# Denominators of block 2 on GpSimd and a re-timed side program in an attention + two-MoE kernel

## The chip, the cores and the metric

The kernel runs on one core of one Trainium2 chip. The metric is the device time of one execution in microseconds (us). Three runs of the kernel before gave 718.23, 719.92 and 720.44 us; the median is 719.92 us.

## What is computed

Three layers follow each other, all in float32; the reference, cut to what matters:

```python
# 1: linear attention, 4 batches x 8 heads x 576 tokens, head size 64, 128 features
proj = x @ w_phi                                   # for q and for k
proj = proj - max(abs(proj), axis=-1)
phi  = concat([exp(proj), exp(-proj)])             # s = 0 and s = 1 below
kv, z = k_phi.T @ v, sum(k_phi)
y = (q_phi @ kv) / (q_phi @ z + 1e-6)              # num / den
# 2: gated MLP over 2304 tokens, d_model 512, d_ff 1536
xn = y / sqrt(mean(y * y, -1) + 1e-6) * rms_g
o  = (silu(xn @ w_gate) * (xn @ w_val)) @ w_out
# 3: soft MoE, 8 experts x 4 slots, over the 2304 rows of o
logits = o @ phi
slots  = experts(softmax(logits, axis=0).T @ o)
out    = softmax(logits, axis=1) @ slots
```

## The kernel before

**Stages of the program.** First all of k and v are reduced to kv and z per batch and head, with the q side of block 0 in between (class Rows). Then comes the main loop: six blocks of 384 tokens. For each block b, twelve steps m compute a gate tile (pg), a value tile (pv) and add three output tiles (acc); every gate and value tile is 12 matmuls, because each operand is split into a high and a low part. Last come the experts (y) and the combination (op).

**The side program.** Beside the MoE of block b run the q side of block b+1 and the slot steps of block b-1, cut into small functions. Each m has three fill points, so a block has fills 0 to 35. Tables of fill numbers say where each function is issued: TURNED1 for the q side of block 1, REDUCED for block 2, ADDED for blocks 3 to 5, PSLOTS for the slot steps. A scheduler then orders the instructions of each engine; from block 2 on `placed` pins VectorE's order to the order of issue.

**Three ways to do the q side.** Turned (block 1): tokens in the rows; the projection (P) is turned by TensorE (T) and exponentiated; pairs of heads give the sums num and the denominators den on TensorE. Reduced (block 2): the projection is qP (two matmuls), GpSimd takes the largest magnitude across partitions (L308), VectorE subtracts it (L312), ScalarE takes both exponentials (L313, L314), and num and den are matmuls again (L223, L251). Added (blocks 3 to 5): num as before, but the denominator is weighted on ScalarE and VectorE (L351, L352) and summed across partitions by GpSimd (L353), one call per head; norm (L371 to L375) divides. num takes, for a pair of heads, first both heads' s = 0, then both heads' s = 1: the two heads write different halves of the rows.

**The mean square.** For blocks 1 and 2 scale makes three one-column matmuls (ssq, L269) from s, the sum of squares, then a reciprocal root, a diagonal dg (L274), and spreads it: for block 1 by a matmul (r, L439), for block 2 by GpSimd (L321). For blocks 3 to 5 GpSimd sums the squares across partitions (total, L381) and transposes on VectorE (L385, L364) make and spread the root. out (L282) multiplies into xraw, and split_block casts it to xnh and xnl (L121, L124) for the next block's MoE.

**Slot steps** (post): three turns (x2tp), logits (LT), rows (L), dturn (dtp), dispatch (sps), combine (VectorE) and cturn (ctp).

**Memory.** Block 0's loop still converts the last nine weight pieces in a pool of its own (conv); block 2's q pool is opened when block 1's loop begins.

Of the kernel before, what the change touches and what calls it, by code (L numbers as in the profile page):

```python
# [7 lines left out]
F32 = mybir.dt.float32  # L8
# [3 lines left out]
ALU = mybir.AluOpType  # L12
# [4 lines left out]
NB, NH, SEQ, HD, DF = 4, 8, 576, 64, 128  # L17
NT, DM, DFF = 2304, 512, 1536
# [17 lines left out]
CEVERY = 3  # L36
PSLOTS = [1, 4, 7, 12, 14, 16, 18, 20, 24]
REDUCED = [0, 0, 2, 3, 5, 6, 4, 8, 7, 11, 12, 9, 14, 12, 17, 18, 15, 20, 18, 23, 24, 27, 30]
ADDED = [-3, -3, -1, 0, 2, 3, 6, 1, 5, 4, 8, 9, 12, 6, 11, 9, 14, 15, 18, 12, 17, 15, 20, 21, 25, 26, 28, 31]
TURNED0 = [2, 8, 14, 20, 12, 15, 20, 26, 28, 33]  # L40
TURNED1 = [0, 7, 14, 21, 6, 13, 20, 26, 29, 31]

# [25 lines left out]
def tile_kernel(ctx: ExitStack, tc: tile.TileContext, q2T, qT, kT, v, wbd, wg, wv, wo, rmsg, phi, w1, w2, consts, out):  # L68
# [30 lines left out]
    qctx = ctx.enter_context(ExitStack())  # L99
# [6 lines left out]
    ident = cst[:, 0:128]  # L106
# [98 lines left out]
    class Q:  # L205
# [35 lines left out]
        def attend(self, c):  # L241
# [22 lines left out]
            self.next_kv(c)  # L264

        def scale(self):
            ssq = self.psum("ssq", [128, TPB])
            for i in range(TPB):
                PE.matmul(out=ssq[:, i:i + 1], lhsT=self.s[:, 128 * i:128 * i + 128], rhs=ones_sb[:, 0:1], start=True, stop=True)  # L269
            ms = self.sp.tile([128, TPB], F32, tag="ms", name="ms", bufs=1)  # L270
            DVE.tensor_scalar(out=ms, in0=ssq, scalar1=1.0 / DM, scalar2=1e-6, op0=ALU.mult, op1=ALU.add)
            rsqrt(self.sp, ms)
            dg, r = self.spare()
            DVE.tensor_tensor(out=dg.rearrange("p (i t) -> p i t", i=TPB),  # L274
                              in0=ident.rearrange("p (o t) -> p o t", o=1).to_broadcast([128, TPB, 128]),
                              in1=ms.rearrange("p (i o) -> p i o", o=1).to_broadcast([128, TPB, 128]), op=ALU.mult)
            self.r = self.spread(r, dg)

# [5 lines left out]
    class Reduced(Q):  # L284
# [31 lines left out]
        def spare(self):  # L316
            e = self.sp.tile([128, 2, BLK], F32, tag="e", name="dg", bufs=4)
            return e[:, 0], e[:, 1]

        def spread(self, r, dg):  # L320
            POOL.partition_all_reduce(r, dg, channels=128, reduce_op=bass_isa.ReduceOp.add)  # L321
            return r

        def begin(self):
            self.pair = {}
            for h in range(3):
                self.load(h)

        def steps(self):
            def first():  # L330
                self.split(0)
                self.load(3)

            f = [lambda h=h: self.feature(h) for h in range(NH)]
            a = [lambda c=c: self.attend(c) for c in range(4)]
            g = [lambda h=h: self.exps(h) for h in range(NH)]
            s = [first, *(x for c in range(4) for x in (f[2 * c], f[2 * c + 1], g[2 * c], g[2 * c + 1], a[c])), self.scale, self.out]
            return sorted(zip(REDUCED, s), key=lambda x: x[0])

    class Added(Reduced):  # L340
# [14 lines left out]

        def few(self, name, x, scale, add):

            f = self.sp.tile([128, BLK // 32, 1], F32, tag=name, name=name, bufs=1)
            DVE.tensor_scalar(out=f, in0=x.rearrange("p (b j) -> p b j", j=32)[:, :, 0:1], scalar1=scale, scalar2=add, op0=ALU.mult, op1=ALU.add)
            return f  # L360

        def many(self, out, f):

            DVE.transpose(out=out.rearrange("p (b j) -> p b j", j=32), in_=f.to_broadcast([128, BLK // 32, 32]))  # L364

        def norm(self, c):
# [9 lines left out]
            self.square(c, y, e[0][:, 1])  # L376

        def total(self):
            e = self.sp.tile([128, 2, BLK], F32, tag="e", name="ss", bufs=4)
            self.ss = e[:, 0], e[:, 1]  # L380
            POOL.partition_all_reduce(self.ss[0], self.s, channels=128, reduce_op=bass_isa.ReduceOp.add)  # L381

        def scale(self):
            ss, self.r = self.ss
            DVE.transpose(out=self.r, in_=ss)  # L385
            ms = self.few("ms", self.r, 1.0 / DM, 1e-6)
            f = ms.rearrange("p b o -> p (b o)")
            rsqrt(self.sp, f, BLK // 32)
            self.many(self.r, ms)

# [12 lines left out]
    class Turned(Q):  # L403
# [29 lines left out]
        def spare(self):  # L433
            e = self.sp.tile([128, 2, 2, BLK], F32, tag="e", name="dg", bufs=self.bufs["e"])
            return e[:, 0, 0], None

        def spread(self, r, dg):
            r = self.psum("r", [128, BLK])
            PE.matmul(out=r, lhsT=ones_sb[:, 0:1].to_broadcast([128, 128]), rhs=dg, start=True, stop=True)  # L439
            return r  # L440

# [3 lines left out]

        def steps(self, at, attend, end, lag=2):


            r, pr = [], {}

            def p(c, i):
                pr[c, i] = self.project(c, i)

            for c in range(4):
                for i in range(TPB):
                    r.append((at[c] + i, lambda c=c, i=i: p(c, i)))
                    r.append((at[c] + i + lag, lambda c=c, i=i: self.turn(c, i, pr[c, i])))
                r.append((attend[c], lambda c=c: self.attend(c)))
            r += [(end[0], self.scale), (end[1], self.out)]
            return sorted(r, key=lambda x: x[0])  # L460
# [283 lines left out]
    with ExitStack() as p2:  # L744
# [483 lines left out]
```

## Time and profile before

| | |
|---|---|
| runs (us) | 718.23, 719.92, 720.44 |
| profiled execution | 719.95 us, of which the span of the program on the core is 718.0 us |
| TensorE busy | 702.5 us, 98% of the span |
| VectorE, ScalarE, GpSimd busy | 453.2, 340.8, 125.3 us |
| granted TensorE clock, mean of the span | 0.994 |

PE is TensorE, PEld its weight loads, DVE VectorE, ACT ScalarE, POOL GpSimd, SP the queue that issues DMAs; L223 is line 223 of the kernel before. In a timeline a row stands for a run of like instructions: start, duration from the first one's start to the last one's end, engine, line, operation, out<-in, shapes, count, and in brackets the idle time before it and who ended it. A float32 matmul is recorded as two instructions, so four num matmuls of 384 columns read as x8. Matmuls overlap: the start of the next row tells more than the end of this one.

### The profile page before, as it was taken

How to read it: one execution, taken by the hardware profiler on the slowest of the kernel's cores; microseconds unless marked ns; L12 is line 12 of the kernel's file. 1: busy time of each engine (PE TensorE's matmuls, PEld its weight loads, DVE VectorE, ACT ScalarE, POOL GpSimd, SP SyncE). 2: the span in 40 equal slices, each digit the busy share in tenths (PEclk: the TensorE clock that was granted, in tenths of full speed). 3: DMA queues.
4: the chain of work that ended last, by engine and by line, in shares of the span. 5: the costliest groups of instructions: out<-in, count | busy, mean ns of one | idle time of the engine just before them, and what ended most of it. 6: DMA issues, size and time to landing. Idle time of an engine off the chain costs nothing.

```text
span 718.0 us, 11949 instructions
## 1 busy us (share of the span) xinstructions
PE 702.5 (98%) x4729; PEld 574.2 (80%) x4729; DVE 453.2 (63%) x889; ACT 340.8 (47%) x715; POOL 125.3 (17%) x66
## 2 busy tenths in 40 slices
PE   7999999999999999999999999999999999999995
PEld 4666667888889888888879888899887999988443
DVE  4889995999575564656766667766666663243313
ACT  4878886788444554454441555414444231112103
POOL 0000000000002110125542244432443400000100
PEclk9999999999999999999999999999999999999998
DMA  6755534551011100100000100001000057467898
GB/s 227 269 183 180 186 128 147 188 187 60 1 64 44 34 23 12 39 23 22 23 1 9 44 23 24 1 9 35 21 1 1 9 234 294 176 252 283 316 365 287
DMA packets 25143, 79.43 MB, mean 111 GB/s; under 512 B 2688, under 2 KB 13376, under 8 KB 18688
## 3 DMA queue, kind: packets, MB, share of 16 engines
q1 hardware_dynamic: 24720, 77.52, 30.6%
q10 hardware_dynamic: 368, 1.15, 0.5%
q8 instruction: 37, 0.61, 0.3%
q14 instruction: 18, 0.15, 0.1%
HBM read 71.99 MB, written 6.67 MB: 110 GB/s over the span
## 4 chain that ended last, share of the span: by engine, by line
PE 95%; ACT 2%; DMA 1%; DVE 1%; issue 0%; SPq 0%; ACTq 0%
PE pv L954 22%; PE pg L954 21%; PE acc L979 7%; PE acc L980 7%; PE acc L981 7%; PE kacc L573 5%; PE num L223 5%; PE P L528 3%; PE kacc L582 3%; PE y L1116 2%; PE y L1100 2%; PE o L474 1%; PE P L414 1%; DMA wraw<-in_wo_dram 1%; PE x2tp L763 1%; PE den L251 1%
## 5 line engine op out<-in xcount | busy, mean ns | idle before, releaser
L954 PE MATMUL pv<-xnh,wv 128*128 128x384 f32 x576 | 152.8, 346 | 0.0
L954 PE MATMUL pg<-xnh,wg 128*128 128x384 f32 x576 | 150.2, 342 | 0.3 <-ACT xnh L121 0.3
L954 PEld LDWEIGHTS pv<-xnh,wv 128*128 128x128 f32 x576 | 102.6, 188 | 12.3 <-issue 7.5
L308 POOL PARTITION_ALL_REDUCE qe<-qe x32 | 51.3, 1602 | 334.5 <-ACT qe L307 334.5
L954 PEld LDWEIGHTS pg<-xnh,wg 128*128 128x128 f32 x576 | 104.6, 188 | 5.7 <-ACT xnh L121 0.7
L954 PE MATMUL pg<-xnl,wg 128*128 128x384 f32 x288 | 97.5, 339 | 0.0
L954 PE MATMUL pv<-xnl,wv 128*128 128x384 f32 x288 | 97.5, 339 | 0.0
L979 PE MATMUL acc<-wo,hh 128*128 128x512 f32 x216 | 88.9, 412 | 0.0
L980 PE MATMUL acc<-wo,hh 128*128 128x512 f32 x216 | 85.7, 397 | 0.0
L981 PE MATMUL acc<-wo,hl 128*128 128x512 f32 x216 | 85.5, 396 | 0.0
L962 DVE SCALAR_TENSOR_TENSOR t<-t,pg 128x384 f32<-128x384 f32 x72 | 39.7, 551 | 71.1 <-ACT t L961 70.9
L121 ACT CAST hh<-t 128x384 fp32r<-128x384 f32 x72 | 36.9, 513 | 96.2 <-PE acc L980 74.9
L124 DVE TENSOR_TENSOR hl<-t,hh 128x384 fp32r<-128x384 f32 x72 | 40.6, 564 | 53.5 <-ACT hh L121 44.4
L353 POOL PARTITION_ALL_REDUCE qe<-qe x24 | 61.9, 2626 | 71.3 <-DVE qe L352 41.8
L961 ACT ACTIVATE t<-pg 128x384 f32<-128x384 f32 x72 | 35.3, 490 | 66.0 <-PE pg L954 65.9
L966 DVE TENSOR_TENSOR t<-t,pv 128x384 f32<-128x384 f32 x72 | 39.5, 548 | 30.1 <-PE pv L954 29.5
L954 PEld LDWEIGHTS pg<-xnl,wg 128*128 128x128 f32 x288 | 54.0, 188 | 0.5 <-DVE xnl L124 0.3
L954 PEld LDWEIGHTS pv<-xnl,wv 128*128 128x128 f32 x288 | 54.1, 188 | 0.4 <-issue 0.3
L981 PEld LDWEIGHTS acc<-wo,hl 128*128 128x128 f32 x216 | 40.6, 188 | 10.0 <-DVE hl L124 0.3
L979 PEld LDWEIGHTS acc<-wo,hh 128*128 128x128 f32 x216 | 40.7, 189 | 7.9 <-ACT hh L121 0.9
L980 PEld LDWEIGHTS acc<-wo,hh 128*128 128x128 f32 x216 | 40.7, 189 | 6.4
L573 PE MATMUL kacc<-kp,vt 128*64 128x256 f32 (+1 forms) x320 | 41.2, 393 | 2.3 <-ACT kp L550 2.3
(218 smaller groups left out, 1060.9 us busy)
## 6 DMA issues: line engine op xcount, KB each, us to landing
eu<-in_w_dram SPq DMA_DIRECT2D x32, 1024.0 KB, 6.3
wraw<-in_wg_dram SPq DMA_DIRECT2D x6, 1024.0 KB, 4.8
wraw<-in_wv_dram SPq DMA_DIRECT2D x6, 1024.0 KB, 5.5
wraw<-in_wo_dram SPq DMA_DIRECT2D x6, 1024.0 KB, 5.1
qraw<-in_qT_dram SPq DMA_DIRECT2D x32, 192.0 KB, 2.3
vt<-in_v_dram SPq DMA_DIRECT2D x18, 256.0 KB, 3.3
out_dram<-ob SPq DMA_DIRECT2D x18, 256.0 KB, 2.9
raw<-in_kT_dram SPq DMA_DIRECT2D x17, 256.0 KB, 3.1
```

The source lines that it names most:

```text
L121: ACT.copy(out=hi, in_=src)
L124: (lo_eng or POOL).tensor_tensor(out=lo, in0=src, in1=hi.bitcast(F32), op=ALU.subtract)
L223: PE.matmul(out=num[64 * hh:64 * hh + 64, t0:t1], lhsT=kvt[b][:, 2 * c + hh, s, 0:HD], rhs=e[hh][:, s, t0:t1], start=s == 0, stop=s == 1, ...
L308: POOL.partition_all_reduce(e[:, 0], e[:, 1], channels=128, reduce_op=bass_isa.ReduceOp.absmax)
L353: POOL.partition_all_reduce(e[hh][:, 1], u, channels=128, reduce_op=bass_isa.ReduceOp.add)
L573: PE.matmul(out=kva[o0:o0 + 64, hh // 2], lhsT=self.vt[r0:r1, h], rhs=kp[r0:r1, hh].rearrange("p s f -> p (s f)"), start=first and hh < 2, ...
L954: PE.matmul(out=p, lhsT=w[:, a, c], rhs=x, start=n == 0, stop=n == 11)
L962: DVE.scalar_tensor_tensor(out=t, in0=t, scalar=1.0, in1=g, op0=ALU.add, op1=ALU.mult)
L966: DVE.tensor_tensor(out=t, in0=t, in1=wide("v", m, xs), op=ALU.mult)
L979: PE.matmul(out=acc[i], lhsT=hh[:, s], rhs=w[:, 0], start=m == 0, stop=False)
L980: PE.matmul(out=acc[i], lhsT=hh[:, s], rhs=w[:, 1], start=False, stop=False)
L981: PE.matmul(out=acc[i], lhsT=hl[:, s], rhs=w[:, 0], start=False, stop=m == MF - 1)
```

## The change

The denominators and squares of block 2 are done as in blocks 3 to 5 (class Reduced loses its own schedule, Added takes block 2 too, and its first steps run in block 0's last fills). Block 1's sum of squares is spread by one matmul with a matrix of ones, followed by the same VectorE transposes as in the other blocks, and gets a step of its own (total, at fill 27). In ADDED three steps move: the subtraction and exponentials of the second head of pairs 1, 2 and 3 go from fills 8, 14, 20 to 7, 13, 19. PADDED replaces PSLOTS and puts logits, dispatch and cturn at the fills of the attention sums (9, 15, 21); the last block has PLAST. Block 1's projections go from fills 7, 14, 21 to 3, 10, 17, the turns stay. `placed` now holds from block 1 on. Block 2's q pool takes the place of the conversion's pool, two steps before block 0 ends.

```diff
-PSLOTS = [1, 4, 7, 12, 14, 16, 18, 20, 24]
-REDUCED = [0, 0, 2, 3, 5, 6, 4, 8, 7, 11, 12, 9, 14, 12, 17, 18, 15, 20, 18, 23, 24, 27, 30]
-ADDED = [-3, -3, -1, 0, 2, 3, 6, 1, 5, 4, 8, 9, 12, 6, 11, 9, 14, 15, 18, 12, 17, 15, 20, 21, 25, 26, 28, 31]
+PADDED = [1, 3, 6, 9, 11, 11, 15, 17, 21]
+PLAST = [2, 2, 2, 6, 9, 9, 15, 12, 15]
+ADDED = [-3, -3, -1, 0, 2, 3, 6, 1, 5, 4, 7, 9, 12, 6, 11, 9, 13, 15, 18, 12, 17, 15, 19, 21, 25, 26, 28, 31]
-TURNED1 = [0, 7, 14, 21, 6, 13, 20, 26, 29, 31]
+TURNED1 = [0, 3, 10, 17, 6, 13, 20, 26, 27, 29, 31]
...
+        def total(self):
+            self.ss = self.spare()
+            POOL.partition_all_reduce(self.ss[0], self.s, channels=128, reduce_op=bass_isa.ReduceOp.add)
+
         def scale(self):
-            ssq = self.psum("ssq", [128, TPB])
-            for i in range(TPB):
-                PE.matmul(out=ssq[:, i:i + 1], lhsT=self.s[:, 128 * i:128 * i + 128], rhs=ones_sb[:, 0:1], start=True, stop=True)
-            ms = self.sp.tile([128, TPB], F32, tag="ms", name="ms", bufs=1)
-            DVE.tensor_scalar(out=ms, in0=ssq, scalar1=1.0 / DM, scalar2=1e-6, op0=ALU.mult, op1=ALU.add)
-            rsqrt(self.sp, ms)
-            dg, r = self.spare()
-            DVE.tensor_tensor(out=dg.rearrange("p (i t) -> p i t", i=TPB),
...
-            self.r = self.spread(r, dg)
+            ss, self.r = self.ss
+            DVE.transpose(out=self.r, in_=ss)
+            ms = self.few("ms", self.r, 1.0 / DM, 1e-6)
+            f = ms.rearrange("p b o -> p (b o)")
+            rsqrt(self.sp, f, BLK // 32)
+            self.many(self.r, ms)
...
     class Turned(Q):
...
-        def spread(self, r, dg):
-            r = self.psum("r", [128, BLK])
-            PE.matmul(out=r, lhsT=ones_sb[:, 0:1].to_broadcast([128, 128]), rhs=dg, start=True, stop=True)
-            return r
+        def total(self):
+            ssq = self.psum("ssq", [128, BLK])
+            PE.matmul(out=ssq, lhsT=ones_sb[:, 0:1].to_broadcast([128, 128]), rhs=self.s, start=True, stop=True)
+            self.ss = ssq, self.spare()[1]
...
-                    r.append((at[c] + i + lag, lambda c=c, i=i: self.turn(c, i, pr[c, i])))
+                    r.append((at[c] + i + lag[c], lambda c=c, i=i: self.turn(c, i, pr[c, i])))
                 r.append((attend[c], lambda c=c: self.attend(c)))
-            r += [(end[0], self.scale), (end[1], self.out)]
+            r += zip(end, (self.total, self.scale, self.out)[-len(end):])
...
-        qnext = q.steps(TURNED1[0:4], TURNED1[4:8], TURNED1[8:], lag=3)
+        qnext = q.steps(TURNED1[0:4], TURNED1[4:8], TURNED1[8:], lag=[3, 7, 7, 7])
...
             if blk == 1:
-                tctx.close()
                 q1ctx.close()
-                qp = pool(qctx, "qp", side="right")
-                q = Reduced(qp, ps, 2, {"misc": 3})
-                q.begin()
-                qsteps = q.steps()
                 sp = pool(pctx, "post", side="right")
...
-            for n, f in zip(PSLOTS, steps):
+            for n, f in zip(PADDED if blk < NBLK - 1 else PLAST, steps):
                 plan[n].append(f)
...
-                    if blk>1:
+                    if blk > 0:
                         placed(f, DVE.engine)
...
-                if m == MF - 3 and 3 <= blk + 2 < NBLK:
+                if m == MF - 3 and blk + 2 < NBLK:
+                    if blk == 0:
+                        tctx.close()
+                        qp = pool(qctx, "qp")
                     q = Added(qp, ps, blk + 2, {"misc": 3})
```

few and many (a handful of values from a transposed tile, and their spreading by a transpose) move from Added to the base class unchanged; Reduced loses spread and steps.

How the instructions stand on an engine, at three places. Numbers behind a name tell its copies apart; lines of the changed kernel are smaller by about 30.

TensorE near the end of block 0's loop, before: ssq is block 1's mean square, r its spreading, acc2 the third output tile, pg and pv the next gate and value tile.

```order
L979 MATMUL acc2_1482<-wo4_1975,hh_2180 128x512
L980 MATMUL acc2_1482<-wo4_1975,hh_2180 128x512
L981 MATMUL acc2_1482<-wo4_1975,hl_2181 128x512
L269 MATMUL ssq_2270<-small_77,s_1675 128x1 x3
L954 MATMUL pg_2293<-xnh0_1422,wg5_2070 128x384 x2
...
L954 MATMUL pv_2309<-xnh2_1430,wv5_2139 128x384
L439 MATMUL r_2291<-dg_2289,small_77 128x384
L954 MATMUL pv_2309<-xnh2_1430,wv5_2139 128x384
```

The same place in the changed kernel:

```order
L952 MATMUL acc1_1481<-wo4_1981,hl_2181 128x512
L950 MATMUL acc2_1482<-wo4_1981,hh_2180 128x512
L410 MATMUL ssq_2243<-s_1695,small_77 128x384
L951 MATMUL acc2_1482<-wo4_1981,hh_2180 128x512
L952 MATMUL acc2_1482<-wo4_1981,hl_2181 128x512
L925 MATMUL pg_2300<-xnh0_1422,wg5_2088 128x384 x2
```

The wide ssq stands two output matmuls earlier than the three narrow ones did, and r is gone.

TensorE in block 1's loop, at the second attention sum of block 2, before (num and den of one pair of heads, then the first logits, LT):

```order
L954 MATMUL pg_2714<-xnl3_2353,wg2_1224 128x384
L223 MATMUL num_2730<-qe_2540,kv1_796 64x384
L223 MATMUL num_2730<-qe_2656,kv1_796 64x384
...
L251 MATMUL den_2735<-qe_2540,kv1_796 32x192 x2
L251 MATMUL den_2735<-qe_2656,kv1_796 32x192 x2
...
L773 MATMUL LT_2761<-x2T_2473,phi_sb_76 32x128
```

The same pair in the changed kernel:

```order
L925 MATMUL pg_2661<-xnl3_2360,wg2_1224 128x384
L223 MATMUL num_2677<-qe_2487,kv1_796 64x384
L223 MATMUL num_2677<-qe_2587,kv1_796 64x384
...
L744 MATMUL LT_2692<-x2T_2495,phi_sb_76 32x128
L744 MATMUL LT_2692<-x2T_2547,phi_sb_76 32x128
```

Left out are the second rows of num and den (s = 1). The eight den matmuls are gone; the logits of the slot steps follow the second pair directly.

VectorE in block 2's loop, around the subtraction of the second head of pair 1 (qe<-qe; xraw is the division by the denominator, hl the low part of the hidden tile, x2T a turned slot tile), before:

```order
L765 COPY x2T_3515<-x2tp_3510 128x512
L375 TENSOR_TENSOR xraw_3401<-xraw_3401,qe_3306 128x384
L297 TENSOR_TENSOR qx_3487<-qraw_3301,qx_3487 64x384
L124 TENSOR_TENSOR hl_3527<-t_3475,hh_3526 128x384
L312 TENSOR_TENSOR qe_3459<-qe_3459 128x384
```

In the changed kernel:

```order
L359 TENSOR_TENSOR xraw_3367<-xraw_3367,qe_3272 128x384
L306 TENSOR_TENSOR qx_3453<-qraw_3267,qx_3453 64x384
L736 COPY x2T_3467<-x2tp_3462 128x512
L321 TENSOR_TENSOR qe_3425<-qe_3425 128x384
L124 TENSOR_TENSOR hl_3496<-t_3441,hh_3495 128x384
```

The subtraction now stands ahead of hl, with the slot copy x2T between it and qx.

## Rows read from the trace of the kernel before

**Rows 1.** The page, part 1: busy time, share of the span, instructions of each engine.

```profile
PE 702.5 (98%) x4729; PEld 574.2 (80%) x4729; DVE 453.2 (63%) x889; ACT 340.8 (47%) x715; POOL 125.3 (17%) x66
```

**Rows 2.** Windows, stages 0 to 4: length, busy PE, PEld, DVE, ACT, POOL (count), clock, DMA.

```profile
118.25:211.65 93.40, 93.22 (x569) 82.50 (x570) 74.34 (x123) 63.08 (x120) 0.00 (x0) 1.00 0.32 113
211.65:304.99 93.34, 93.04 (x562) 80.70 (x561) 54.48 (x109) 47.13 (x111) 14.99 (x9) 1.00 0.10 29
304.99:396.03 91.04, 91.04 (x492) 79.12 (x491) 58.63 (x123) 37.84 (x83) 35.83 (x17) 1.00 0.05 15
396.03:488.38 92.35, 92.26 (x525) 80.73 (x525) 63.47 (x136) 40.35 (x94) 35.60 (x17) 1.00 0.07 20
488.38:579.87 91.49, 91.40 (x492) 79.02 (x491) 60.48 (x128) 38.03 (x84) 35.92 (x17) 1.00 0.05 13
```

**Rows 3.** Timeline of TensorE, stage 1, the first pair of heads of block 2.

```profile
234.80 1.51 PE L223 MATMUL num<-qe,kv 128*64 128x384 f32 x8
236.24 0.86 PE L251 MATMUL den<-qe,kv 128*32 128x192 f32 x16
237.03 0.62 PE L954 MATMUL pv<-xnh,wv 128*128 128x384 f32 x2
```

**Rows 4.** Timeline of TensorE, around ssq and r at the ends of stages 0 and 1.

```profile
202.66 0.39 PE L979 MATMUL acc<-wo,hh 128*128 128x512 f32 x1
...
203.13 0.40 PE L981 MATMUL acc<-wo,hl 128*128 128x512 f32 x1
203.71 0.80 PE L269 MATMUL ssq<-small,s 128*128 128x1 f32 x6 [0.18 <-DVE s L233]
204.37 0.60 PE L954 MATMUL pg<-xnh,wg 128*128 128x384 f32 x2
...
207.95 0.88 PE L439 MATMUL r<-dg,small 128*128 128x384 f32 x2
...
293.66 0.83 PE L269 MATMUL ssq<-small,s 128*128 128x1 f32 x6 [0.30 <-DVE s L233]
294.35 0.60 PE L954 MATMUL pv<-xnh,wv 128*128 128x384 f32 x2
```

**Rows 5.** Timeline of VectorE: block 1's last s, and a transpose of block 3's squares.

```profile
203.01 0.56 DVE L233 TENSOR_TENSOR s<-s,e 128x384 f32<-128x384 f32 x1
...
388.98 0.58 DVE L385 STREAM_TRANSPOSE ss<-ss 128x384 f32<-128x384 f32 x1 [0.66 <-POOL ss L381]
```

**Rows 6.** Windows for the tile num alone, stages 1 to 4: length, PE, PEld, ACT, clock.

```profile
211.65:304.99 93.34, 6.05 (x32) 1.95 (x32) 1.92 (x4) 1.00 0.10 29
304.99:396.03 91.04, 7.40 (x32) 2.93 (x32) 1.89 (x4) 1.00 0.05 15
396.03:488.38 92.35, 7.99 (x64) 4.76 (x64) 1.89 (x4) 1.00 0.07 20
488.38:579.87 91.49, 7.37 (x32) 2.93 (x32) 1.90 (x4) 1.00 0.05 13
```

**Rows 7.** Timeline of TensorE, stage 2, the sum of pair 1.

```profile
337.26 1.92 PE L223 MATMUL num<-qe,kv 128*64 128x384 f32 x8
```

**Rows 8.** Timeline of VectorE, stage 2, before and during that sum.

```profile
334.84 0.56 DVE L297 TENSOR_TENSOR qx<-qraw,qx 64x384 fp32r<-64x384 f32 x1
335.80 0.56 DVE L124 TENSOR_TENSOR hl<-t,hh 128x384 fp32r<-128x384 f32 x1 [0.41 <-ACT hh L121]
336.28 0.55 DVE L312 TENSOR_TENSOR qe<-qe 128x384 f32<-128x384 f32 x1
...
339.87 2.02 DVE L312 TENSOR_TENSOR qe<-qe 128x384 f32<-128x384 f32 x1
```

**Rows 9.** Timeline of GpSimd, stage 2: a maximum, and a pair's denominator sums.

```profile
333.27 1.54 POOL L308 PARTITION_ALL_REDUCE qe<-qe  x1 [2.63 <-ACT qe L307]
339.59 5.23 POOL L353 PARTITION_ALL_REDUCE qe<-qe  x2 [4.78 <-DVE qe L352]
```

**Rows 10.** Timeline of ScalarE, stage 2: the second head's second exponential.

```profile
337.76 0.51 ACT L314 ACTIVATE qe<-qe 128x384 f32<-128x384 f32 x1
```

More of the change, by code (lines that the diff above doesn't have):

```diff
@@ L264, in attend, with few, many @@
             self.next_kv(c)
-        def scale(self):
-            ssq = self.psum("ssq", [128, TPB])
-            for i in range(TPB):
-                PE.matmul(out=ssq[:, i:i + 1], lhsT=self.s[:, 128 * i:128 * i + 128], rhs=ones_sb[:, 0:1], start=True, stop=True)
-            ms = self.sp.tile([128, TPB], F32, tag="ms", name="ms", bufs=1)
-            DVE.tensor_scalar(out=ms, in0=ssq, scalar1=1.0 / DM, scalar2=1e-6, op0=ALU.mult, op1=ALU.add)
-            rsqrt(self.sp, ms)
-            dg, r = self.spare()
-            DVE.tensor_tensor(out=dg.rearrange("p (i t) -> p i t", i=TPB),
-                              in0=ident.rearrange("p (o t) -> p o t", o=1).to_broadcast([128, TPB, 128]),
-                              in1=ms.rearrange("p (i o) -> p i o", o=1).to_broadcast([128, TPB, 128]), op=ALU.mult)
-            self.r = self.spread(r, dg)
+        def few(self, name, x, scale, add):
+            f = self.sp.tile([128, BLK // 32, 1], F32, tag=name, name=name, bufs=1)
+            DVE.tensor_scalar(out=f, in0=x.rearrange("p (b j) -> p b j", j=32)[:, :, 0:1], scalar1=scale, scalar2=add, op0=ALU.mult, op1=ALU.add)
+            return f
+        def many(self, out, f):
+            DVE.transpose(out=out.rearrange("p (b j) -> p b j", j=32), in_=f.to_broadcast([128, BLK // 32, 32]))
+        def total(self):
+            self.ss = self.spare()
+            POOL.partition_all_reduce(self.ss[0], self.s, channels=128, reduce_op=bass_isa.ReduceOp.add)
+        def scale(self):
+            ss, self.r = self.ss
[4 more added lines that the diff above has]
+            self.many(self.r, ms)
         def out(self):
@@ L316, in spare @@
         def spare(self):
-            e = self.sp.tile([128, 2, BLK], F32, tag="e", name="dg", bufs=4)
+            e = self.sp.tile([128, 2, BLK], F32, tag="e", name="ss", bufs=4)
             return e[:, 0], e[:, 1]
-        def spread(self, r, dg):
-            POOL.partition_all_reduce(r, dg, channels=128, reduce_op=bass_isa.ReduceOp.add)
-            return r
         def begin(self):
@@ L327, in begin @@
                 self.load(h)
[L329 to L338, printed above, removed]
     class Added(Reduced):
@@ L354, in attend @@
             self.next_kv(c)
[L356 to L364, printed above, removed]
         def norm(self, c):
@@ L376, in norm @@
             self.square(c, y, e[0][:, 1])
[L378 to L389, printed above, removed]
         def steps(self):
@@ L433, in spare @@
         def spare(self):
-            e = self.sp.tile([128, 2, 2, BLK], F32, tag="e", name="dg", bufs=self.bufs["e"])
-            return e[:, 0, 0], None
-        def spread(self, r, dg):
-            r = self.psum("r", [128, BLK])
-            PE.matmul(out=r, lhsT=ones_sb[:, 0:1].to_broadcast([128, 128]), rhs=dg, start=True, stop=True)
-            return r
+            e = self.sp.tile([128, 2, 2, BLK], F32, tag="e", name="ss", bufs=self.bufs["e"])
+            return e[:, 0, 0], e[:, 0, 1]
+        def total(self):
+            ssq = self.psum("ssq", [128, BLK])
+            PE.matmul(out=ssq, lhsT=ones_sb[:, 0:1].to_broadcast([128, 128]), rhs=self.s, start=True, stop=True)
+            self.ss = ssq, self.spare()[1]
         def begin(self):
@@ L444, in begin, with steps @@
                 self.load(c)
-        def steps(self, at, attend, end, lag=2):
+        def steps(self, at, attend, end, lag=[2] * 4):
             r, pr = [], {}
```

## The prediction

> **What bounds the kernel now.** I read the busy times first. TensorE is busy 702.5 of 718.0 us, 98% [rows 1]: other engines can matter only where TensorE waits for them or where work leaves it. Then the windows view, cut where each MoE block's first gate matmul starts [rows 2]. I call the stretch of MoE block b stage b; it carries the q side of block b+1. Stages 1 to 4 hold the same MoE matmuls and the same slot steps, and yet take 93.34, 91.04, 92.35 and 91.49 us. In stage 2 TensorE is busy for the whole stage, so by that view there is nothing to win in it. The reader should distrust this: a matmul that stands between its neighbours waiting for an operand still counts as busy, because matmuls overlap.
>
> The same windows for the tile num alone show it [rows 6]. Four attention sums cost 6.05 us in stage 1 and 7.40, 7.99 and 7.37 us in stages 2 to 4: the same matmuls, 1.35 + 1.94 + 1.32 = 4.61 us more. One of them in the timeline: 1.92 us [rows 7], where one in stage 1 takes 1.51 [rows 3]. Its operands tell why. GpSimd's maximum for the second head is ready at 333.27 + 1.54 = 334.81 [rows 9]. VectorE has finished qx at 334.84 + 0.56 = 335.40, but waits for hh, does hl at 335.80, and only then subtracts at 336.28 [rows 8]; the second head's last exponential ends at 337.76 + 0.51 = 338.27 [rows 10], 1.0 us after the sum began at 337.26 [rows 7].
>
> Taking these waits out, stages 2 to 4 would be 89.69, 90.41 and 90.17 us, 90.09 on average. That is what a stage costs with the denominators on GpSimd and no waiting inside the sums.
>
> **The change part by part.**
>
> *Block 2's denominators (stage 1).* Removed from TensorE: four den groups, each 236.24 to 237.03 = 0.79 us [rows 3], 3.16 together; the three squares matmuls, 294.35 - 293.66 = 0.69, and the 0.30 before them [rows 4]. That makes 4.15 us by parts. By stages it is 93.34 - 90.09 = 3.25 us. I take the second: it counts what the parts do not, the return from a sum straight to a weight matmul and the first qP of a stage. Added: 8 sums on GpSimd, a pair of them 5.23 us [rows 9], and one total; GpSimd goes from 14.99 to about 35.8 us, as in stages 2 to 4 [rows 2], hidden under 90 us of TensorE. ScalarE loses the copies of the denominators, VectorE gets transposes: about the 58.63 us it has in stage 2, hidden too. If that cover went, each late operand would show as a stretched num, as above.
>
> *Second heads' subtractions sooner (stages 2 to 4).* VectorE's new order does the subtraction ahead of hl, so in the example it starts when qx and one moved copy are done, between 335.4 and about 336.1 instead of at 336.28. The two exponentials then follow without the tanh that stood between them, about 1.05 us for both, so the last ends between 337.0 and 337.7. The sum's second half, which reads it, begins near 337.26 + 1.51 / 2 = 338.0. So the wait goes. hl comes half a microsecond later, for an output matmul that stands behind the sum and a whole value tile: nothing. I count all of the 4.61 us. Ends: 0 (another operand is late next: the first head's exponentials, or ScalarE's queue) to 4.61.
>
> *Slot steps beside the sums.* The same instructions, on every engine, at other places. The logits now stand right behind the second sum, and the maximum on VectorE right behind a subtraction that took 2.02 us instead of 0.55, when it came 0.28 us after a GpSimd sum's start [rows 8, 9]. The turned d needs that maximum and an exponential, but TensorE has twelve value and nine output matmuls in between: 12 gate and 7 value matmuls take 207.95 - 204.37 = 3.58 us, 0.19 each, and an output matmul 0.235 [rows 4], so 12 x 0.19 + 9 x 0.235 = 4.4 us. I price it at 0, with 0 to 0.4 us per stage as ends. In the last stage no q side is left and nothing waits: 0.
>
> What that 2.02 us row says of the port: the subtraction was held for about 1.5 us, less than the sum's length (a pair takes 5.23), and VectorE idles over 30 us of such a stage. By the row the price is nothing on TensorE. The Trainium skill, SBUF — State Buffer, Who interferes with whom, says that a VectorE instruction with two SBUF inputs and a GpSimd instruction that reads SBUF exclude each other for a whole instruction, the loser blocking fully. By that rule the sum would be another one, and it is a rival below.
>
> *Block 1's squares by one matmul pair (end of stage 0).* Removed: three small matmuls, 204.37 - 203.71 = 0.66 us, and the pair r (0.88 at 207.95); added: one pair of r's very shape, which cancels r [rows 4]. But the last s is written at 203.01 + 0.56 = 203.57 [rows 5], so TensorE, which started ssq at 203.71, can start the new pair no sooner. The new order puts the pair two output matmuls earlier: (203.13 - 202.66) = 0.47 us of work [rows 4] that filled the wait now stands behind it. Net 0.66 - 0.47 = 0.19 us saved, and an idle of some 0.8 us to be seen before ssq. VectorE behind it gets two transposes of 0.58 [rows 5] for a multiplication and the pair's 0.88, about even; TensorE's order has two qP matmuls at the seam as filler. Ends: 0.66 saved to 0.3 lost.
>
> *qT's early loads for block 2.* They go into the conversion's old memory. They stand on SP's queue behind the last weight load and ahead of the kv load, which waits for block 1's last den; so nothing late is in front of them. VectorE takes the two qx before block 1's last sum; an idle engine's work: 0. The earlier projections (3, 10, 17 for 7, 14, 21) only reorder: 0.
>
> *Sum.* Four stages at 90.09: 360.36 for 368.22 us, -7.86. Stage 0: -0.19. For new waits behind the moved slot steps and at seams I put +0.5, between the ends 0 and 1.6. Together -7.55 us on the profiled execution's 719.95, which is the median of the runs shown (719.92) to within 0.03: 712.4 us. With the four stages at the best of the three clean values (89.69, -9.46) and stage 0 at -0.66 it is 709.8; with the worst (90.41, -6.58), +0.3 and +1.6 it is 715.3.
>
> **Rivals.** A change of 0.3% (2.2 us) is about what a measurement of this kernel tells from none.
>
> *The sums still wait (chance 0.12).* If the second head's exponentials come late for another reason (ScalarE's queue, GpSimd's busy queue), stages 2 to 4 stay, and stage 1 becomes one like them, say the 91.04 of stage 2, 2.30 less: 719.95 - 2.3 - 0.2 = 717.4. For it: the tanh and hh stand in ScalarE's queue at the same place. Against: the maximum was there 1.5 us before it was used.
>
> *A new wait at the moved steps (0.10).* Either the turned d or the seam at block 1 costs TensorE some 0.6 us in each of four stages, 2.6 us more: 715.0. For it: VectorE's 2.02 us row in front of the maximum. Against: over 4 us of matmuls in between.
>
> *GpSimd holds VectorE (0.04), the slower side.* Place: stages 1 to 4, where sums on GpSimd run beside two-input VectorE steps. If the two excluded each other wholly, a stage would last their busy times together: 58.63 + 35.83 = 94.46 in stages 1 and 2, 63.47 + 35.60 = 99.07, 60.48 + 35.92 = 96.40 [rows 2], 384.4 us for 368.2, so 736 us. It decides once more than some 10 us of such exclusion reaches TensorE. Against: stage 2 ran in 91.04 with this same sum of 94.46, which total exclusion forbids, and one step in that stretch was held 1.5 us only. This is the rule of the Trainium skill, SBUF — State Buffer, Who interferes with whom, taken strictly.
>
> **Numbers.** Forecast 0.74, the rivals as given. The range reaches from 710.2, near the forecast's best end, to 715.8, past its worst end and the second rival; the first and third lie outside it, 0.16. Faster by over 0.3%: 0.90 (forecast, second rival, part of the first). Within: 0.06 (the rest of the first, whose 2.5 us is at the bound). Slower: 0.04.
>
> **What would show it.** Right: no den in stage 1, GpSimd near 36 us there, num near 6 us in each of stages 1 to 4, these stages near 90 us each, an idle of about 0.8 us before the new ssq. Wrong: num still above 7 us with the second head's exponential ending over 0.7 us into the sum; idle or stretched dtp, LT or first gate matmuls; a VectorE step held for a whole GpSimd sum with TensorE idle behind it.

## The result, and the profile after

The changed kernel takes 712.72 us (median of 5 runs, 710.75 to 713.75) beside 718.23 us for the kernel before in the same session (5 runs, 717.06 to 720.44): a ratio of 0.9918, with a 95% interval of 0.989 to 0.9947. That is 5.5 us less; the forecast was 712.4 us, 7.55 less. The profiled execution took 713.63 us with a span of 711.8.

The page, part 1, to be held against [rows 1]:

```profile
PE 693.4 (97%) x4653; PEld 569.4 (80%) x4653; DVE 464.8 (65%) x911; ACT 332.2 (47%) x691; POOL 147.7 (21%) x74
```

TensorE is busy 9.1 us less and still sets the time. GpSimd has 22.4 us more to do: block 2's eight sums and one total, in place of the one call that spread block 2's root. The windows for stages 0 to 4 answer to [rows 2] and have its columns (length, busy PE, PEld, DVE, ACT, POOL with counts, clock, DMA):

```profile
118.38:212.27 93.89, 92.81 (x564) 81.95 (x564) 75.17 (x125) 63.02 (x121) 0.00 (x0) 1.00 0.34 116
212.27:301.70 89.43, 89.40 (x492) 78.25 (x491) 59.25 (x125) 38.28 (x85) 37.18 (x17) 1.00 0.07 22
301.70:391.79 90.09, 89.87 (x493) 78.23 (x492) 61.50 (x128) 38.62 (x86) 36.11 (x17) 1.00 0.07 20
391.79:483.47 91.68, 90.04 (x525) 80.56 (x524) 65.69 (x136) 40.14 (x94) 35.36 (x17) 1.00 0.07 20
483.47:573.50 90.03, 89.80 (x492) 78.20 (x492) 61.50 (x128) 37.81 (x84) 36.10 (x17) 1.00 0.08 25
sum 455.12, PE 451.91 PEld 397.20 DVE 323.11 ACT 217.86 POOL 144.76; mean PE 90.38 PEld 79.44 DVE 64.62 ACT 43.57 POOL 28.95
```

Against [rows 2] that is +0.49, -3.91, -0.95, -0.67 and -1.46: together -6.50 us. Two stages stand out. Stage 0 became longer. In stage 3 the length exceeds TensorE's busy time by 91.68 - 90.04 = 1.64 us, which before was only 0.09: there TensorE now waits openly. The same windows for the tile num, stages 1 to 4, answer to [rows 6]:

```profile
212.27:301.70 89.43, 6.04 (x32) 2.06 (x32) 1.83 (x4) 1.00 0.07 22
301.70:391.79 90.09, 6.04 (x32) 2.06 (x32) 1.82 (x4) 1.00 0.07 20
391.79:483.47 91.68, 6.25 (x64) 4.41 (x64) 1.83 (x4) 1.00 0.07 20
483.47:573.50 90.03, 6.04 (x32) 2.06 (x32) 1.83 (x4) 1.00 0.08 25
```

The waits inside the sums are gone: 18.33 us in stages 2 to 4 for 22.76. The sum of pair 1 in stage 2, which the prediction took as its example [rows 7 to 10], shows how. VectorE's subtraction, ScalarE's two exponentials and TensorE's sum, in their timelines:

```profile
333.06 0.56 DVE L321 TENSOR_TENSOR qe<-qe 128x384 f32<-128x384 f32 x1
333.53 0.55 DVE L124 TENSOR_TENSOR hl<-t,hh 128x384 fp32r<-128x384 f32 x1
...
333.65 0.53 ACT L322 ACTIVATE qe<-qe 128x384 f32<-128x384 f32 x1 [0.94 <-DVE qe L321]
334.21 0.52 ACT L323 ACTIVATE qe<-qe 128x384 f32<-128x384 f32 x1
...
334.39 1.51 PE L223 MATMUL num<-qe,kv 128*64 128x384 f32 x8
```

The subtraction starts 1.33 us before the sum, where it started 0.98 us before it [rows 7, 8], and hl comes behind it. The second exponential ends at 334.73, only 0.34 us into the sum, where it ended 1.0 us into it. The table of TensorE's waits has what is late instead:

```profile
PE qP L313 <- DVE qx L306: 2.1, 3, 1.6
...
PE ssq L410 <- DVE s L233: 0.7, 1, 0.7
PE P L385 <- ACT e L402: 0.4, 2, 0.2
```

(us in total, times, the longest.) The first line holds the 1.64 us of stage 3 and two waits of a quarter of a microsecond.

### The profile page after: what moved, and what is told of

Read it like the earlier page. It is cut to its first block, busy times and chain, and to the rows that moved or that the text cites. A ratio compares the mean times of both kernels' runs of the same rounds, so it can differ in the third digit from the quotient of the medians.

```text
span 711.8 us, 11799 instructions
## 1 busy us (share of the span) xinstructions
PE 693.4 (97%) x4653; PEld 569.4 (80%) x4653; DVE 464.8 (65%) x911; ACT 332.2 (47%) x691; POOL 147.7 (21%) x74
## 4 chain that ended last, share of the span: by engine, by line
PE 89%; ACT 4%; DVE 3%; DMA 1%; issue 1%; SPq 0%; ACTq 0%
PE pv L925 20%; PE pg L925 19%; PE acc L950 7%; PE acc L951 7%; PE acc L952 7%; PE kacc L544 5%; PE num L223 4%; PE P L499 3%; PE kacc L553 3%; PE y L1085 2%; PE y L1069 2%; PE o L445 2%; PE P L385 1%; DMA wraw<-in_wo_dram 1%; PE qP L313 1%; PE x2tp L734 1%
## 5 line engine op out<-in xcount | busy, mean ns | idle before, releaser
L317 POOL PARTITION_ALL_REDUCE qe<-qe x32 | 51.9, 1620 | 310.4 <-ACT qe L316 307.7
L347 POOL PARTITION_ALL_REDUCE qe<-qe x32 | 83.1, 2646 | 79.0 <-DVE qe L346 79.0
L322 ACT ACTIVATE qe<-qe 128x384 f32<-128x384 f32 x32 | 16.8, 526 | 70.5 <-DVE qe L321 70.5
```

Source lines behind the costliest of these rows:

```text
L317: POOL.partition_all_reduce(e[:, 0], e[:, 1], channels=128, reduce_op=bass_isa.ReduceOp.absmax)
L347: POOL.partition_all_reduce(e[hh][:, 1], u, channels=128, reduce_op=bass_isa.ReduceOp.add)
```

## The experiments

Whole times are a blunt tool here: the stretch ahead of stage 0, which no edit touches, took between 115.47 and 118.49 us in the profiles (the last section shows where they part). The stage lengths of the profiles are therefore compared, cut as in [rows 2], where the kernel before stands. In us; the time is a median where there are several runs.

| kernel | stage 0 | 1 | 2 | 3 | 4 | sum | time, ratio to before |
|---|---|---|---|---|---|---|---|
| changed kernel | 93.89 | 89.43 | 90.09 | 91.68 | 90.03 | 455.12 | 712.72, 0.9918 |
| e3: before, new subtractions | 93.44 | 93.35 | 89.69 | 90.38 | 90.14 | 457.00 | 712.67, 0.9922 [0.9897, 0.9946] |
| e1: old subtractions | 93.44 | 92.89 | 93.37 | 94.69 | 93.30 | 467.69 | 725.70, 1.0091 [1.0064, 1.0119] |
| e5: denominators alone | 93.33 | 91.23 | 91.50 | 92.35 | 91.44 | 459.85 | 717.58, 0.9984 [0.9969, 1.0] |
| e2: old slot steps | 93.30 | 89.94 | 90.16 | 90.36 | 90.16 | 453.92 | 711.29, 0.9891 [0.9871, 0.9911] |
| e4: second turn later | 93.45 | 89.45 | 90.09 | 89.94 | 90.03 | 452.96 | 709.86, 0.9872 [0.985, 0.9894] |
| e6: no second sums, block 4 | 93.50 | 89.38 | 90.04 | 90.10 | 90.05 | 453.07 | 709.26, one run |
| e7: old projections | 92.93 | 89.42 | 90.09 | 91.71 | 90.03 | 454.18 | 710.18, one run |
| e8: squares two later | 92.80 | 90.52 | 90.04 | 91.66 | 90.05 | 455.07 | 714.41, one run |
| e9: both repairs | 92.94 | 89.43 | 90.08 | 89.92 | 90.03 | 452.40 | 709.63, 0.9878 [0.986, 0.9896] |
| e10: changed kernel again | 93.26 | 89.42 | 90.02 | 91.67 | 90.03 | 454.40 | 712.48, 0.991 [0.9894, 0.9927] |

### The subtractions: alone, left out, and left out with the slot steps

**e3**, the kernel before with the new row ADDED and nothing else (block 2 does not use this table).

```diff
-ADDED = [-3, -3, -1, 0, 2, 3, 6, 1, 5, 4, 8, 9, 12, 6, 11, 9, 14, 15, 18, 12, 17, 15, 20, 21, 25, 26, 28, 31]
+ADDED = [-3, -3, -1, 0, 2, 3, 6, 1, 5, 4, 7, 9, 12, 6, 11, 9, 13, 15, 18, 12, 17, 15, 19, 21, 25, 26, 28, 31]
```

> The kernel before with only the second heads' subtractions moved to fills 7, 13, 19. Theory A: num falls from 7.40, 7.99, 7.37 us in stages 2 to 4 to about 6.05, 6.2, 6.05, so 4.4 us less than before, a ratio near 0.994. Theory B: num stays above 7 and the time within 0.3% of before.

Stages 2 to 4 became 89.69, 90.38 and 90.14 us, 4.67 less than in [rows 2] (the prediction, which only took the surplus of num off, had 89.69, 90.41 and 90.17). The window of num in stage 2, which is [rows 6]'s 7.40 without the wait:

```profile
302.26:391.95 89.69, 6.04 (x32) 2.06 (x32) 1.84 (x4) 1.00 0.05 16
```

So the stretched matmuls of [rows 6], counted as busy, were waits, and one fill is all that they lacked. The medians differ by 6.9 us, more than the five stages' 4.62. In the two profiles, whose spans are 710.6 and 718.0 us, the rest stands ahead of stage 0, which the edit does not touch: that stretch is 115.47 us long in e3's, 118.25 in that of before [rows 2].

**e1**, the changed kernel with the old row ADDED (the edit of e3 the other way round).

> The changed kernel with the second heads' subtractions back at fills 8, 14, 20; all else stays. Theory A (the sooner subtractions cured the sums): num goes from 6.04, 6.04, 6.25, 6.04 us in stages 1 to 4 back to some 7.4, 7.4, 8.0, 7.4, about 6 us more, so some 718 to 719 us. Theory B (moving the slot steps out of VectorE's way cured them): num stays below 6.4 in every stage and the time within 1 us of the changed kernel's 712.7.

It came out slower than the kernel before, and 12.57 us longer than the changed kernel over the five stages. That is far more than the 4.61 that the old places had cost, and twice the 6 us of theory A. The windows of the tile num and of the tile sps, stage 2:

```profile
304.82:398.19 93.37, 8.30 (x32) 2.56 (x32) 1.88 (x4) 1.00 0.07 19
...
304.82:398.19 93.37, 2.10 (x6) 0.28 (x6) 0.73 (x1) 1.00 0.07 19
```

Now num is at 8.30, 2.26 over the changed kernel's 6.04, and dispatch, which had been put in between the parts of a waiting sum, is at 2.10 where the changed kernel has 1.06: together these are the stage's 3.28 us (93.37 for 90.09). The cause is in VectorE's timeline ahead of the sum of pair 3 in stage 2, with that sum in TensorE's:

```profile
363.94 0.25 DVE L784 TENSOR_REDUCE rm<-c 128x3 f32<-128x96 f32 x1
...
366.88 0.24 DVE L795 TENSOR_TENSOR c<-c,c 128x96 fp32r<-128x96 f32 x1
...
367.50 1.17 DVE L355 STREAM_TRANSPOSE qe<-qe 64x384 f32<-64x384 f32 x2
...
371.81 0.55 DVE L321 TENSOR_TENSOR qe<-qe 128x384 f32<-128x384 f32 x1
...
371.86 0.86 PE L223 MATMUL num<-qe,kv 128*64 128x384 f32 x2
372.97 0.54 PE L223 MATMUL num<-qe,kv 128*64 128x384 f32 x2 [0.25 <-ACT qe L322]
```

The moved slot softmax (nine steps, 363.94 to 367.12) stands ahead of the division of the pair before, whose transposes start 4.4 us before the sum; the subtraction behind it starts as the sum does.

**e5**, the changed kernel with the old ADDED and with the slot steps where they were:

```diff
-PADDED = [1, 3, 6, 9, 11, 11, 15, 17, 21]
-PLAST = [2, 2, 2, 6, 9, 9, 15, 12, 15]
-ADDED = [-3, -3, -1, 0, 2, 3, 6, 1, 5, 4, 7, 9, 12, 6, 11, 9, 13, 15, 18, 12, 17, 15, 19, 21, 25, 26, 28, 31]
+PADDED = [1, 4, 7, 12, 14, 16, 18, 20, 24]
+PLAST = PADDED
+ADDED = [-3, -3, -1, 0, 2, 3, 6, 1, 5, 4, 8, 9, 12, 6, 11, 9, 14, 15, 18, 12, 17, 15, 20, 21, 25, 26, 28, 31]
```

> The changed kernel with the old places of the subtractions and the old places of all slot steps: block 2's denominators on GpSimd and block 1's squares are all that is left of the change. Theory A (the parts do not depend on each other): old subtractions cost what they cost beside the moved slot steps, stages 1 to 4 stay at 92.9, 93.4, 94.7 and 93.3 us, the tile num at 8 us or more in each, the whole near 725. Theory B (the old subtractions are only so late because the slot steps were moved away from the matmuls ahead of the sums): stages 2 to 4 are those of the kernel before, 91.0, 92.3 and 91.5 us with num at 7.4 to 8.0; stage 1 is one like them, 91 to 91.5; the whole near 717.5.

Theory B is right, stage by stage and in the whole time. VectorE at the same place in stage 2, and the sum:

```profile
360.25 1.17 DVE L355 STREAM_TRANSPOSE qe<-qe 64x384 f32<-64x384 f32 x2
...
365.83 0.55 DVE L321 TENSOR_TENSOR qe<-qe 128x384 f32<-128x384 f32 x1
366.30 0.24 DVE L784 TENSOR_REDUCE rm<-c 128x3 f32<-128x96 f32 x1
...
366.67 1.65 PE L223 MATMUL num<-qe,kv 128*64 128x384 f32 x7
```

Here the transposes run 6.4 us before the sum and the slot softmax comes behind the subtraction, which starts 0.84 us ahead of the sum. The parts of the change thus depend on each other: with the old subtractions, moving the slot steps costs 467.69 - 459.85 = 7.84 us; with the new ones 1.20 (against e2), half of which is stage 0. And the denominators on GpSimd alone give stage 1 only 91.23, 2.11 less than in [rows 2], because its sums then wait as well:

```profile
209.53:300.76 91.23, 7.30 (x32) 2.98 (x32) 1.88 (x4) 1.00 0.07 21
```

That is num in stage 1: 1.26 us over the 6.04 of the changed kernel.

### The slot steps and the wait in stage 3

**e2**, the changed kernel with the old slot fills (the first four lines of e5's edit, ADDED left new).

> The changed kernel with the slot steps at their old fills (1, 4, 7, 12, 14, 16, 18, 20, 24, also in the last block). Theory A: num stays near 6.0 in stages 1 to 4, and the 1.64 us wait of qP in stage 3 goes, because the slot copy x2T is no longer ahead of the subtraction: 711 us. Theory B: num is back above 7 us in stages 2 to 4 and the time some 4 us higher, near 717.

Against it the changed kernel's stage 1 is 0.51 us shorter and its stage 3 is 1.32 longer; stages 2 and 4 differ by 0.07 and 0.13. The moved steps as such are worth half a microsecond in one stage, and in another they made a new wait. Here it is: the changed kernel in stage 3, from the subtraction of block 4's third head to the projection qP of its fifth, in the timelines of VectorE, GpSimd, ScalarE and TensorE.

```profile
409.88 3.05 DVE L346 SCALAR_TENSOR_TENSOR qe<-qe,kv 128x192 f32<-128x192 f32 x4
412.85 0.68 DVE L736 COPY x2T<-x2tp 128x512 f32<-128x512 f32 x1
...
413.91 1.71 DVE L321 TENSOR_TENSOR qe<-qe 128x384 f32<-128x384 f32 x1
...
417.77 1.25 DVE L306 TENSOR_TENSOR qx<-qraw,qx 64x384 fp32r<-64x384 f32 x1
...
411.02 5.03 POOL L347 PARTITION_ALL_REDUCE qe<-qe  x2 [4.82 <-DVE qe L346]
417.69 1.54 POOL L317 PARTITION_ALL_REDUCE qe<-qe  x1 [1.63 <-ACT qe L316]
...
415.66 0.53 ACT L322 ACTIVATE qe<-qe 128x384 f32<-128x384 f32 x1 [4.53 <-DVE qe L321]
...
419.16 0.41 PE L313 MATMUL qP<-qx,ws 128*128 128x384 f32 x1 [1.64 <-DVE qx L306]
```

Read it along VectorE. Four weightings (L346), the last of them stretched by GpSimd's first sum; the copy of the second turn; the multiplication by the value tile; then the subtraction. The two sums take 5.03 us, so the second starts near 413.5, the subtraction half a microsecond behind it, and it takes 1.71 us for 0.55. The exponentials, the copy of qP and the cast for qx behind it on ScalarE are late, and qx itself, 0.08 us after the start of GpSimd's next maximum, takes 1.25 for 0.56 on top. TensorE has nothing left and waits 1.64 us.

**e4** moves only that copy, by one fill:

```diff
-PADDED = [1, 3, 6, 9, 11, 11, 15, 17, 21]
+PADDED = [1, 4, 6, 9, 11, 11, 15, 17, 21]
```

> The changed kernel with the second slot turn back at fill 4 (PADDED 1, 4, 6, ...). VectorE then has the subtraction ahead of the copy x2T, so it starts before the second GpSimd sum does. Theory C (the 1.64 us wait of qP in stage 3 comes from VectorE steps held at the starts of GpSimd calls, with x2T in the way): the wait falls below 0.3 us, stage 3 from 91.7 to about 90.1, the time to about 711. Theory D (the wait is the general load of VectorE in the block that spans two batches): the wait stays over 1 us.

Stage 3 is 89.94, 1.74 shorter; no other of stages 1 to 4 moved by over 0.02. The same stretch, VectorE and GpSimd:

```profile
408.66 3.05 DVE L346 SCALAR_TENSOR_TENSOR qe<-qe,kv 128x192 f32<-128x192 f32 x4
...
412.09 0.55 DVE L321 TENSOR_TENSOR qe<-qe 128x384 f32<-128x384 f32 x1
412.56 0.68 DVE L736 COPY x2T<-x2tp 128x512 f32<-128x512 f32 x1
...
414.82 0.56 DVE L306 TENSOR_TENSOR qx<-qraw,qx 64x384 fp32r<-64x384 f32 x1
...
409.81 5.21 POOL L347 PARTITION_ALL_REDUCE qe<-qe  x2 [4.84 <-DVE qe L346]
414.92 1.85 POOL L317 PARTITION_ALL_REDUCE qe<-qe  x1
```

Without the copy ahead of it the subtraction starts just ahead of the second sum and is done in 0.55 us; qx ends 414.82 + 0.56 - 408.66 = 6.7 us after the weightings began instead of 417.77 + 1.25 - 409.88 = 9.1. With the copy repaired, the moved slot steps gain 1.11 us over e2 in stages 1 to 4.

**e6** asks whether GpSimd's reading is what holds VectorE. For block 4 alone:

```diff
-                POOL.partition_all_reduce(e[hh][:, 1], u, channels=128, reduce_op=bass_isa.ReduceOp.add)
+                if self.blk == 4:
+                    POOL.memset(e[hh][:, 1], 1.0)
+                else:
+                    POOL.partition_all_reduce(e[hh][:, 1], u, channels=128, reduce_op=bass_isa.ReduceOp.add)
```

> The changed kernel, but for block 4 (stage 3) GpSimd writes a constant in place of the eight sums of the denominators, so block 4's attention is not normalised; nothing else is moved on any engine. Theory C (while GpSimd's sum reads, VectorE's steps with two SBUF inputs are held, and that is what makes the second turn's copy, the subtraction and qx late in stage 3): the product ahead of the second sum is back from 1.77 to 0.4 us, the subtraction behind it from 1.71 to 0.55, TensorE's 1.64 us before qP near the eighth of stage 3 is gone, the stage 91.68 to about 90.0. Rival (VectorE is late there only because the moved copy and the addition stand ahead of the subtraction in its order): the wait stays at 1 us or more, the stage at 91 or more.

VectorE and GpSimd in the same stretch, in VectorE's unchanged order:

```profile
406.83 1.70 DVE L346 SCALAR_TENSOR_TENSOR qe<-qe,kv 128x192 f32<-128x192 f32 x4
408.44 0.68 DVE L739 COPY x2T<-x2tp 128x512 f32<-128x512 f32 x1
...
410.40 0.55 DVE L321 TENSOR_TENSOR qe<-qe 128x384 f32<-128x384 f32 x1
...
407.93 0.42 POOL L348 MEMSET qe<- 128x384 f32 x1 [4.79 <-DVE qe L346]
408.65 0.42 POOL L348 MEMSET qe<- 128x384 f32 x1 [0.30 <-DVE qe L346]
```

The four weightings take 1.70 us for 3.05, the subtraction 0.55 for 1.71, and the stage 90.10 for 91.68. The order alone does no harm; the hold does. A constant is also quicker to write than a sum is to take (0.42 for about 2.5 us), so the run tells that the sums hold VectorE, not which of their phases does.

### Block 1: the projections and the squares (stage 0)

**e7**, the projections back, the turns where they are:

```diff
-TURNED1 = [0, 3, 10, 17, 6, 13, 20, 26, 27, 29, 31]
+TURNED1 = [0, 7, 14, 21, 6, 13, 20, 26, 27, 29, 31]
...
-        qnext = q.steps(TURNED1[0:4], TURNED1[4:8], TURNED1[8:], lag=[3, 7, 7, 7])
+        qnext = q.steps(TURNED1[0:4], TURNED1[4:8], TURNED1[8:], lag=[3, 3, 3, 3])
```

> The changed kernel with block 1's projections back at fills 7, 14 and 21 and every turn three fills behind. Theory D (the early projections stand behind turns and wait for ScalarE's exponentials, which is why stage 0 did not get its 0.19 us): the waits of P for e are gone, stage 0 at 93.2 or less instead of 93.45 to 93.9. Rival (stage 0's loss is the squares' wait alone): stage 0 stays at 93.4 or more.

Stage 0 is 92.93, and in e9, which has the same edit, 92.94; the seven profiles with the early projections (all but e8's) have 93.26 to 93.89. In two places of the changed kernel a projection right behind a turn shows that it waits, here the first, in TensorE's timeline:

```profile
156.99 0.38 PE L400 MATMUL T<-cst,qpr 128*128 128x128 f32 x2
157.57 0.70 PE L385 MATMUL P<-wbd_f,qraw 128*128 128x256 f32 x2 [0.20 <-ACT e L402]
```

So the edit that the prediction passed over as one that only reorders costs 0.3 us or more (93.26 - 92.93), in six of the seven profiles under 0.6. How long a projection waits differs between the profiles; in each with the early places at least one starts 0.2 us or more later behind its turn than the others do.

**e8**, the squares behind the output matmuls:

```diff
-TURNED1 = [0, 3, 10, 17, 6, 13, 20, 26, 27, 29, 31]
+TURNED1 = [0, 3, 10, 17, 6, 13, 20, 26, 29, 29, 31]
```

> The changed kernel with block 1's squares pair two fills later, behind the output matmuls that stood ahead of the old ssq. Theory E (the pair stands ahead of its operand and the 0.47 us of output matmuls that covered the wait stand behind it): the 0.66 us of idle time before ssq is gone, stage 0 shorter by 0.3 to 0.6 us. Rival (the work only changes places, and block 2's first qP waits for what VectorE does behind the squares): stage 0 shorter, stage 1 longer by as much, or both unchanged.

Stage 0 became 1.09 us shorter and stage 1 1.09 longer: 183.32 us for both, as in the changed kernel's first profile. Beside e10, where both take 182.68, the later squares lose 0.64. The rival is right in its kind, but not in its place: not qP waits. The wait ahead of ssq is down to 0.2 us, but the input of block 1's MoE, which the squares scale, is ready later: among TensorE's waits is now one of 0.3 us of stage 1's gate matmuls for its low part (xnl), which the changed kernel does not have. VectorE's four xnl steps, from 213.03 to 215.70 us, now run into GpSimd's first maximum of block 2, which starts at 213.82.

### Both repairs, beside the changed kernel

**e9** has e4's and e7's edits, **e10** is the changed kernel once more.

> The changed kernel with both repairs: the second turn's copy one fill later and block 1's old projections. If the two are independent, as theories C and D have it: stage 0 at 92.9 us, stages 1 to 4 as with the copy alone (89.45, 90.09, 89.94, 90.03), 2.3 us less than the changed kernel over the five stages together (452.5 for 455.1 by the profiled stages, the 0.4 us by which stage 0 differs between runs aside). Rival (the old projections move the stages behind them as well): the five stages at 454 or more.

> The changed kernel itself, beside the one with both repairs on the same chip. By theory C stage 3 shows 91.7 us and the 1.64 us before qP again; by theory D stage 0 is between 93.4 and 93.9 us with P waiting for e. If either was an accident of one profile, stage 3 is at 90 us or stage 0 at 93 us here.

e9 is borne out: its five stages take 452.40 us where 452.5 were expected. Of e10 one half is: the changed kernel shows its 91.67 in stage 3 again. The other half is not: its stage 0 takes 93.26 us, below the 93.4 to 93.9 expected, and no wait of P is in the list. So a good part of what stage 0 lost in the first profile was of that execution alone. A shorter delay is left: e10's projection behind the turn at 172.60 us starts 0.43 us after it, that behind the turn at 156.18 only 0.22 after. That is 0.21 of the 0.33 us which e10's stage 0 has over e7's; where the rest arises is not shown. On the same chip e9 took 709.63 us, the changed kernel 712.48 and the kernel before 719.30: the ratios' intervals (0.986 to 0.9896 and 0.9894 to 0.9927) just overlap. e9 and e4 are the fastest versions here; their difference, 0.5 us in stage 0, is too small for the whole times.

## Why the prediction was right, and where it was off

**The sums' waits (-4.61).** Right in cause and size. The stretched num of [rows 6] were waits; num lost 4.43 us in stages 2 to 4, and e3 has 4.67 from this edit alone. A small error in size: stage 3's sums are cut in two where the batch changes (x64 for x32) and have 6.25 us without a wait, not the 6.05 that the prediction took for all, so num could lose only some 4.4 of the 4.61. What the prediction did not see is that the edit was needed by the others: e1 shows 12.57 us more without it.

**Block 2's denominators (-3.25).** Stage 1 lost 3.91, of which 0.51 belongs to the slot steps (e2), so 3.40: the value by stages was nearer than the 4.15 by parts. But 1.29 of it (91.23 in e5, 89.94 in e2) is there only because the new subtractions also serve block 2; the term was right for the change as a whole, not for its part.

**New waits (+0.5, ends 0 and 1.6).** Against e3, in whose stages 2 to 4 TensorE is idle for 0.17 us in all (length less busy time: 0.00, 0.08 and 0.09), the changed kernel's are 0.40 and 1.30 longer and 0.11 shorter: 1.59 us, the very end of the range. This is the term that was mis-sized, and the step that failed is "I price it at 0" for the slot steps. The prediction looked at the steps that moved beside the sums (the logits, the maximum, the turned d) and at the seam, and bounded those. The 0.40 in stage 2 is of the seam, not of the slot steps: e2, with the old fills, has 90.16 us there too, and e5 91.50 for the 91.04 of before. Block 2's input to that stage now comes the way of blocks 3 to 5; which of its steps costs the time is not shown. The 1.30 in stage 3 came from the copy of the second turn, which moved from fill 4 to 3 and was not looked at (the one moved copy that the prediction counts ahead of its example is the third turn's): it pushed a subtraction, itself not moved, from just ahead of the start of a GpSimd sum to just behind it.

**Block 1's squares (-0.19) and projections (0).** The idle time before ssq was forecast at some 0.8 us and is 0.66. What the change does to stage 0 besides the projections, the squares above all, gave more than forecast: 93.40 to 92.93 with the projections left where they were (e7), 0.47 us. The early projections, priced at 0, took back more than all of it in the first profile (stage 0 at +0.49) and 0.33 in the second (-0.14). Pricing them at 0 as a mere change of order is the second step that failed.

**Sum.** Stages 1 to 4 were forecast at -7.86 + 0.5 = -7.36 and gave -6.99; stage 0 was off by 0.68 in the first profile and by 0.05 in the second. So the mechanism was the right one, and over the five stages its gain came out smaller by 0.3 us (e10, 454.40 for 461.62) to 1.1 us (the first profile). That the median of 712.72 lies only 0.3 us from the forecast time is in part luck: the prediction set out from 719.95, but the kernel before had a median of 718.23 in that session. Between medians the gain was 5.5 us there and 6.8 beside e10, not 7.55.

**The rivals.** The sums do not wait (first rival: no). A new wait came (second rival), in one stage, not in four, and at another step. The third, that GpSimd holds VectorE, is true in miniature: 1.64 us, not 16. The prediction had its row, the 2.02 us subtraction [rows 8], read it rightly as a hold of 1.5 us, and set it at nothing because VectorE is idle for 30 us of a stage. Idle time in the mean did not help a step with another engine waiting on it.

## What to carry to other kernels

A matmul can wait and be counted as busy: compare the same tile between stages that hold the same work before believing that an engine at 98% has nothing to give. When steps are moved on an in-order engine, list every one of them, the smallest copy too, with the step that it now stands ahead of and who waits for that; and try such parts together as well as alone, since one part can be what makes another harmless. Where GpSimd reads on-chip memory beside VectorE, put VectorE's urgent steps with two inputs there ahead of the call, or late in it, not right behind its start.

## What the runs showed of the hardware

**How long GpSimd holds VectorE.** The timelines of VectorE and GpSimd in the changed kernel, stages 2 and 3:

```profile
337.00 2.02 DVE L321 TENSOR_TENSOR qe<-qe 128x384 f32<-128x384 f32 x1
336.72 5.23 POOL L347 PARTITION_ALL_REDUCE qe<-qe  x2 [4.79 <-DVE qe L346]
...
430.62 0.55 DVE L321 TENSOR_TENSOR qe<-qe 128x384 f32<-128x384 f32 x1
431.54 0.54 DVE L937 TENSOR_TENSOR t<-t,pv 128x384 f32<-128x384 f32 x1
428.80 5.03 POOL L347 PARTITION_ALL_REDUCE qe<-qe  x2 [5.71 <-DVE qe L346]
```

The subtraction at 337.00 starts 0.28 us into a sum of about 2.6 and ends at 339.02. Had it run its usual 0.55 us at the end, it was held until 338.47, 1.75 us into the call. The one at 430.62 starts 1.82 us into a sum and is not held at all, though the sum still runs. The same holds for the shorter maximum: qx at 417.77 above was held until 418.47, 0.78 us into a call of 1.54. The multiplication at 431.54, which reads the value tile from PSUM, starts right behind the second sum's start (428.80 + about 2.5) and is not held, nor is e4's copy of a turn out of PSUM at 412.56, which starts as close behind its second sum's (409.81 + about 2.5). So in these rows it is the first half to two thirds of a GpSimd call that is exclusive, and only against steps with two inputs in SBUF. The hold goes the other way too: in e4 qx starts at 414.82, just ahead of GpSimd's maximum at 414.92, and now the maximum takes 1.85 us for 1.54.

The Trainium skill, SBUF — State Buffer, Who interferes with whom, has the same division of steps, adds that a GpSimd instruction that only writes does not contend, and lets the one that comes second wait for the whole instruction. Which steps are held agrees with these rows, and e6's constants held nothing; how long does not agree (0.78 of 1.54 us, 1.75 of about 2.6).

**The first 20 us differ between executions.** The windows view from 0 to 20 us shows a mean granted clock of 0.91 in the changed kernel's profile and of 1.00 in e9's. In the changed kernel it was down to 0.71 between 10 and 15 us (at 0.50, the level of 1.2 GHz, from 10 to 12), after five in which TensorE was busy for 2.73, and back at 1.00, the level of 2.4 GHz, behind that; in e3 TensorE was busy for 2.74 of those five and the clock stayed at 1.00, so these rows do not tell why. In the profiles with 0.91 there (before, the changed kernel, e1, e2, e4, e8, e10) stage 0 begins at 117.5 to 118.5 us, in those with 1.00 (e3, e5, e6, e7, e9) at 115.5 to 116.3. These 2 us are as much as the smaller parts of this change, which is why the stages and not the whole times were compared.
